# Four small row vectors loaded through GpSimd's queue, and their PE transpose placed later, in a gated state-space and MLP kernel

## The chip, the cores and the metric

The kernel runs on one core of a Trainium2 chip. Times are device microseconds of one execution. A smaller number, the **span**, runs from the first to the last instruction that the profile shows. The engines are PE (matmul; PEld is its weight load), DVE (vector), ACT (scalar), POOL (GpSimd) and SP (sync, here the main issuer of transfers).

## The reference, cut to what matters

```python
g = sigmoid((x * gate_w).sum(-1))                  # x: 2048 x 640, bf16
# branch A: a diagonal complex recurrence of 640 states along the 2048 steps
dt = exp(log_dt); Lam = Lambda_re + 1j * Lambda_im
Lam_bar = exp(dt * Lam)                            # needs exp, sin and cos of small vectors
B_bar = ((Lam_bar - 1) / Lam)[:, None] * (B_re + 1j * B_im)
h[t] = Lam_bar * h[t-1] + B_bar @ x[t]
a = 2 * real(C @ h) + x * Dskip
# branch B: an MLP of 1728 hidden units
b = gelu(x @ w1 + b1) @ w2 + b2
out = g * a + (1 - g) * b
```

The four small vectors of the title are `Lambda_re`, `Lambda_im`, `log_dt` (640 each) and the first 1664 elements of `b1`.

## The kernel before: the parts concerned

The vectors are loaded as rows of one 128 x 128 tile, 128 elements a row, and PE transposes the tile once, so that each vector lies down the partitions. The transpose borrows PSUM bank 7 before the MLP needs it.

```python
for i, (nm, (r0, src)) in enumerate(ROWS.items()):       # lre, lim, ldt, b1a
    src = src.rearrange("(k p) -> k p", p=128)
    load(nm, "act", "l_" + nm, rows[r0:r0 + src.shape[0], :], src, [nm], prio=-100 + i, dur=0.4)
load("b1b", "act", ...)                                  # the rest of b1, on ACT's queue in both kernels
...
psC = PS[7][:, :].bitcast(BF16)[:, 0:128]
op("cols", "pe", 0.3, list(ROWS) + ["b1b", "ident"], [("bank", 7)], f_cols, prio=13.5)   # the transpose
op("cols1", "dve", 0.2, [("bank", 7)], ["lcol", "b1col"], f_cols1, prio=-1000)           # its copy to SBUF
op("dt", "act", ...)      # exp(log_dt), then on DVE: angles; on ACT: two sines; on DVE: all tables
...
# the first MLP blocks: 42 matmuls, weight block k outermost, bank jf for hidden block jf
op(f"m1_0_{jf}_{k}_{t0}", "pe", ..., [("bank", jf)], f_mm, prio=pe_prio())   # prio 1, 2, 3, ...
op(f"ge_0_{jf}", "act", d_act(512), [("bank", jf), "b1col"], [("gl", 0, jf)], f_ge, prio=10)
...
# elsewhere: the next MLP block takes bank 0 again, so it waits for ge_0_0
```

`op` only registers an instruction. The builder then sorts each engine's instructions with its own estimates of durations (the third argument, `dur`, `lat`): at each step an engine takes the ready one of lowest `prio`. In the traces each engine runs its list in that order: the transpose comes after 13, 18 or 21 matmuls, just as the builder placed it.

## Time and profile before

| | before |
|---|---|
| median of the first three runs | 212.67 us (212.47 to 213.09) |
| span of the profiled run, a later one of 213.45 us | 212.1 us |
| PE busy | 98% |
| DVE busy | 90% |
| ACT busy | 49% |
| GpSimd busy | 2% |

The busy shares say which engine can't be made to wait: PE.

### The profile page before, as it was taken

The numbers are of one execution on the slowest core, as the hardware profiler recorded it, in microseconds if no ns is written. First come the engines' busy times: TensorE is split into PE (matmuls) and PEld (weight loads), VectorE is DVE, ScalarE is ACT, GpSimd is POOL, SyncE is SP. The second block draws the span as 40 slices with busy tenths as digits, with TensorE's granted clock in tenths as the row PEclk, the third lists the DMA queues.
The fourth block names the chain that finished last, engine by engine and source line by source line (L and its number), as shares of the span: only waits on it lengthen the run. The fifth ranks groups of instructions, "written<-read, shape, count | busy, mean of one in ns | idle before, by whom it ended". The sixth has DMA issues, their size and how long they took to land.

```text
span 212.1 us, 2737 instructions
## 1 busy us (share of the span) xinstructions
PE 208.0 (98%) x1088; PEld 104.9 (49%) x1102; DVE 190.1 (90%) x240; ACT 103.0 (49%) x177; POOL 4.2 (2%) x12
## 2 busy tenths in 40 slices
PE   7999999999999999999999999999999999999996
PEld 3444444444564444444464444444446444567775
DVE  2399999999999999999999999899999999499744
ACT  2389556677960353556681063455660027623330
POOL 1000000030000000000000000000010000000000
DMA  5999999999600010075274000004742000005251
GB/s 163 202 279 135 207 171 198 380 222 162 185 12 3 0 49 0 0 85 111 54 59 114 3 0 0 0 2 115 96 96 117 0 3 0 0 0 104 68 140 63
DMA packets 48808, 19.08 MB, mean 90 GB/s; under 512 B 41500, under 2 KB 47772, under 8 KB 48796
## 3 DMA queue, kind: packets, MB, share of 16 engines
q1 hardware_dynamic: 47136, 17.59, 39.7%
q0 software_dynamic: 1600, 1.32, 4.5%
q8 instruction: 8, 0.13, 0.4%
q14 instruction: 4, 0.03, 0.1%
q10 hardware_dynamic: 60, 0.01, 0.0%
HBM read 8.41 MB, written 2.63 MB: 52 GB/s over the span
## 4 chain that ended last, share of the span: by engine, by line
PE 96%; DMA 2%; issue 1%; SPq 0%; DVE 0%
PE ps L662 22%; PE ps L705 20%; PE ps L929 20%; PE ps L978 15%; PE ps L792 7%; PE ps L841 5%; PE ps L640 4%; DMA W1sb<-in_B_w_dram 2%; PE ps L683 1%; PE ps L940 1%; PE ps L806 0%; SPq L333 0%; DVE W1sb L875 0%; PE ps L446 0%
## 5 line engine op out<-in xcount | busy, mean ns | idle before, releaser
L662 PE MATMUL ps<-xT,W1sb 128*128 128x512 bf16 x215 | 47.5, 379 | 0.3
L745 DVE TENSOR_TENSOR_SCAN W<-atab,V 128x1280 bf16<-128x1280 f32 x16 | 44.3, 2812 | 0.3
L705 PE MATMUL ps<-xT,BT 128*128 128x512 bf16 x196 | 43.1, 379 | 0.3 <-issue 0.2
L929 PE MATMUL ps<-Gl,W2sb 128*128 128x512 bf16 (+1 forms) x230 | 42.5, 343 | 0.2
L669 ACT ACTIVATE Gl<-ps,cols 128x512 bf16<-128x512 f32 x44 | 29.9, 694 | 15.5 <-PE ps L662 15.5
L662 PEld LDWEIGHTS ps<-xT,W1sb 128*128 128x128 bf16 x220 | 21.6, 98 | 25.9
L978 PE MATMUL ps<-Hb,CT 128*128 128x512 bf16 x150 | 32.9, 379 | 0.0
L929 PEld LDWEIGHTS ps<-Gl,W2sb 128*128 128x128 bf16 x234 | 22.9, 98 | 19.3
L705 PEld LDWEIGHTS ps<-xT,BT 128*128 128x128 bf16 x200 | 19.5, 98 | 23.7 <-ACT Gt L691 0.4
L714 ACT ACTIVATE U<-ps 128x512 bf16<-128x512 f32 x40 | 23.6, 599 | 14.6 <-PE ps L705 14.5
L947 ACT ACTIVATE E1T<-ps,cols 128x512 bf16<-128x512 f32 (+1 forms) x18 | 9.5, 624 | 36.0 <-PE ps L940 36.0
L978 PEld LDWEIGHTS ps<-Hb,CT 128*128 128x128 bf16 x150 | 14.5, 98 | 17.9 <-DVE V L496 0.6
L986 ACT ACTIVATE E2T<-ps 128x512 bf16<-128x512 f32 x15 | 9.1, 604 | 13.6 <-PE ps L978 13.6
L792 PE MATMUL ps<-W2sb,Gl 128*128 128x320 bf16 x104 | 14.8, 299 | 0.0
L615 DVE SCALAR_TENSOR_TENSOR trf<-xn,gwb 128x640 bf16<-128x640 bf16 x16 | 13.2, 823 | 0.4
L496 DVE TENSOR_TENSOR V<-V,W 128x1280 bf16<-128x1280 bf16 x16 | 12.5, 822 | 0.3
L496 DVE TENSOR_TENSOR Hb<-Hb,V 128x1280 bf16<-128x1280 bf16 x16 | 12.5, 822 | 0.3
L496 DVE TENSOR_TENSOR V<-mr,U 128x2560 bf16<-128x2560 bf16 x8 | 11.9, 1492 | 0.3
L792 PEld LDWEIGHTS ps<-W2sb,Gl 128*128 128x128 bf16 x104 | 10.1, 98 | 4.3 <-issue 0.3
L496 DVE TENSOR_TENSOR Hb<-c,W 128x2560 bf16<-128x2560 bf16 x8 | 11.9, 1491 | 0.2
L496 DVE TENSOR_TENSOR W<-mi,U 128x2560 bf16<-128x2560 bf16 x8 | 11.9, 1484 | 0.0
L496 DVE TENSOR_TENSOR V<-s,W 128x2560 bf16<-128x2560 bf16 x8 | 11.9, 1484 | 0.0
(91 smaller groups left out, 150.8 us busy)
## 6 DMA issues: line engine op xcount, KB each, us to landing
W2sb<-in_B_w_dram SPq DMA_DIRECT2D x1, 2080.0 KB, 8.9
out_dram<-xn SPq DMA_DIRECT2D x3, 640.0 KB, 4.8
xn<-in_A_x_dram POOLq DMA_DIRECT2D x2, 640.0 KB, 7.3
W1sb<-in_B_w_dram SPq DMA_DIRECT2D x3, 256.0 KB, 3.7
trf<-grow SPq DMA_DIRECT2D x3, 256.0 KB, 5.3
xn<-in_A_x_dram SPq DMA_DIRECT2D x1, 640.0 KB, 7.7
W1sb<-in_B_w_dram SPq DMA_DIRECT2D x1, 480.0 KB, 4.6
out_dram<-W1sb SPq DMA_DIRECT2D x3, 160.0 KB, 1.8
```

The source lines that it names most:

```text
L496: return inc("dve", nc.vector.tensor_tensor(out=o, in0=a, in1=b, op=o_))
L615: t = inc("dve", nc.vector.scalar_tensor_tensor(out=scr[:, :], in0=xn[q % 2][:, c, :], scalar=1.0, in1=gwb[:, :], op0=ALU.mult, op1=ALU.mu ...
L662: t = nc.tensor.matmul(PS[bank][:, :], W1sb[:, k, jf * 128:(jf + 1) * 128], xT[q][:, k, :], start=(k == 0), stop=(k == KD - 1))
L669: return inc("act", nc.scalar.activation(Gl[q % 2][:, jf, :], PS[bank][:, :], ACT.Gelu_apprx_tanh, bias=b1col[:, jf:jf + 1]))
L705: t = nc.tensor.matmul(PS[bank][:, :], BT[:, ci, kd, k * 128:(k + 1) * 128], xT[q][:, kd, :], start=(kd == 0), stop=(kd == KD - 1))
L714: return inc("act", nc.scalar.activation(dst, src, ACT.Copy, scale=1.0 if ci == 0 else -1.0))
L745: t = inc("dve", nc.vector.tensor_tensor_scan(out=g[:, ci, :], data0=a, data1=v[:, ci, :], initial=0.0, op0=ALU.mult, op1=ALU.add))
L792: t = nc.tensor.matmul(PS[bank][:, 0:HALF], Gl[q % 2][:, jf, t4 * 128:(t4 + 1) * 128], W2sb[:, jf, cols], start=False, stop=False, skip_gr ...
L841: t = nc.tensor.matmul(PS[bank][:, 0:n], H[b % NHB][:, ci, k, s * 128:(s + 1) * 128], CT[:, ci, k, cols], start=(i == 0), stop=(i == 2 * K ...
L929: t = nc.tensor.matmul(PS[bank][:, 0:t1 - t0], W2sb[:, jf, d * 128:(d + 1) * 128], Gl[q % 2][:, jf, t0:t1], start=(jf == 0), stop=False)
L947: return inc("act", nc.scalar.activation(E1T[:, d, t0:t1], PS[bank][:, 0:t1 - t0], ACT.Identity, bias=cols2[:, 0, d:d + 1]))
L978: t = nc.tensor.matmul(PS[bank][:, :].rearrange("p (s t) -> p s t", s=2), CT[:, ci, k, d * 128:(d + 1) * 128], Hb[:, 2 * (q % 2):2 * (q % ...
```

## The change

The intent, as the edit and the builder's estimates show it: take four transfer issues of 0.31 us each off ACT's queue, where they delay ACT's first table load, and give them to GpSimd, which is idle; and since the builder reckons that GpSimd's loads arrive later, let PE do seven more matmuls before the transpose.

```diff
-            load(nm, "act", "l_" + nm, rows[r0:r0 + src.shape[0], :], src, [nm], prio=-100 + i, dur=0.4)
+            load(nm, "pool", "l_" + nm, rows[r0:r0 + src.shape[0], :], src, [nm], prio=-50 + i, dur=1.0)
...
-        op("cols", "pe", 0.3, list(ROWS) + ["b1b", "ident"], [("bank", 7)], f_cols, prio=13.5)
+        op("cols", "pe", 0.3, list(ROWS) + ["b1b", "ident"], [("bank", 7)], f_cols, prio=20.5)
```

## The prediction

> **What bounds the kernel now.** I read three views, in this order: the chain of work that ended last, the timeline of the first 16 us, and the timeline of DVE over the rest. The chain first:
>
> ```profile
> PE 96%; DMA 2%; issue 1%; SPq 0%; DVE 0%
> ```
>
> 96% of the span is matmuls following one another, and in its ordered form the only pieces that aren't PE or 0.05 us of issue are the start (the first W1 block, issued at 1.26 us, landing at 5.1) and the last DVE evictions. So a change counts only if it moves the first matmul of the main work (5.25 us), opens a hole in PE's stream later, or delays the tail. The change touches the first 10 us, so the timeline of those is next; columns are start us, duration us, engine, line, operation, and in brackets the idle time before it and what ended it:
>
> ```profile
> 1.26 0.14 POOL L398 IOTA st_i<- 128x17 int32 x1
> ...
> 2.20 0.31 ACTq L333 DMA_DIRECT2D rows<-in_A_Lambda_re_dram  x1
> ...
> 3.22 0.32 ACTq L333 DMA_DIRECT2D rows<-in_B_b_dram  x1
> 3.57 1.28 ACT L456 ACT_TABLE_LOAD   x1 [3.57 <-issue]
> ...
> 8.03 0.22 PE L446 MATMUL ps<-ident,rows 128*128 128x128 bf16 x1
> ...
> 8.28 0.19 DVE L451 CAST cols<-ps 128x29 f32<-128x29 bf16 x1 [3.22 <-PE ps L446]
> 8.51 0.21 ACT L456 ACTIVATE dtb<-cols 128x5 bf16<-128x5 f32 x1 [3.65 <-DVE cols L451]
> ...
> 11.19 1.28 ACT L649 ACT_TABLE_LOAD   x1
> ...
> 13.03 3.58 ACT L649 ACTIVATE Gl<-ps,cols 128x512 bf16<-128x512 f32 x6 [0.56 <-PE ps L640]
> ...
> 14.34 1.89 PE L662 MATMUL ps<-xT,W1sb 128*128 128x512 bf16 x8
> ```
>
> The transpose of the row tile (L446, 8.03 us) starts a serial chain: PE, DVE (columns), ACT (exp of log_dt), DVE (angles), ACT (a sine table, two sines), ACT (the gelu table, done at 11.19 + 1.28 = 12.47 us). Only then can ACT evict the first MLP bank. In this kernel it then idles 0.56 us, because the bank itself is finished only at 13.0. That eviction ends near 13.03 + 0.69 = 13.72 us (0.69 is the duration of a gelu eviction), and PE needs its bank again at 14.34 (L662, ninth MLP block, bank 0). So there are **two slacks in series**, 0.56 and 0.62 us, together about 1.2 us from the transpose to a PE stall.
>
> DVE hangs on the same transpose and shows no idle time of note from 8.3 us until these waits:
>
> ```profile
> 84.17 1.49 DVE L496 TENSOR_TENSOR xT<-xT,E2T 128x2560 bf16<-128x2560 bf16 x1 [0.37 <-ACT E2T L986]
> ...
> 134.60 1.49 DVE L496 TENSOR_TENSOR xT<-xT,E2T 128x2560 bf16<-128x2560 bf16 x1 [0.70 <-ACT E2T L986]
> ...
> 183.46 0.17 DVE L626 TENSOR_SCALAR gcol<-gth 128x4 f32<-128x4 f32 x1 [1.43 <-ACT gth L622]
> ```
>
> A late DVE chain therefore stays late until about 84 us, and loses 0.37, 0.70 and 1.43 us of its lateness there.
>
> **What the Trainium skill says.** "DMA: Bandwidth & Descriptors", section "Issuing engines are not separate DMA queues": transfers issued by ScalarE, SyncE or GpSimd run on the same 16 DMA engines, and several issuers save only issue time. The trace fits: the W1 blocks land 3.7 to 3.9 us after issue both while ACT issues its rows and after; the row packets (queue q10, 60 packets in all) are too few to matter. The same page, "Latency and other measured facts", gives about 0.6 us to the first byte for the hardware path and about 1 us for GpSimd's. The trace has it slower: the packet records put the first byte of the first xn load from GpSimd 1.5 us after its issue starts. "Perfetto Trace Analysis", section "DMA Instruction — SWDGE (GPSIMD)", says that a GpSimd transfer's recorded end is the end of descriptor generation, not of data; that fits 0.98 us recorded against 6.5 us to landing here:
>
> ```profile
> cols<-in_B_b_dram POOLq DMA_DIRECT2D x1, 2.5 KB, 6.5
> ```
>
> "ScalarE: Activation LUTs", section "What ACT_TABLE_LOAD costs", gives about 1283 ns for a load, as here, plus a drain of about 1380 ns for a switch; the trace shows no such gap (9.24 + 1.28 = 10.52, next activation 10.60), so I use 1.28.
>
> **The change part by part.**
> *Removed from ACT's queue:* four issues at 0.31 us, from 2.20 to 3.54 us. The exp table load moves up about 1.35 us, and then ACT waits 1.35 us longer for the columns. Worth 0.
>
> *Added to GpSimd's queue:* four issues after the iotas, from about 1.45 us. At 0.77 to 0.98 us each (the four GpSimd issues of this trace), they end at 4.5 to 5.4. The bytes of the last come 0.7 (first xn load) to 2.4 us (the scattered cols load, 3.4 us from issue to first packet) after its descriptors; with half a microsecond to move and signal, rows complete between 5.7 and 8.3 us, best estimate 6.8. In the kernel before, the last row packet is at 5.9 us. GpSimd does nothing else until 43 us, so its time is free.
>
> *The transpose moves back.* The builder sorts each engine's instructions by priority and by its own duration estimates. I take only the order from it. In priority order the transpose passes matmuls 14 to 20. But matmuls 17 and 18 write bank 7, the bank that the transpose borrows, so they can't pass it. The builder's estimate for GpSimd's loads (1.0 each from 1.2, then 2.5) says 7.7, so PE is filled with 14, 15, 16 and 19 to 23: **eight matmuls**, not seven. At 0.2155 us a matmul (20 in 4.32 us in the ordered chain) the transpose is issued at 8.03 + 8 x 0.2155 = 9.75 us. That is 1.5 us after even the late bound of the landing, so PE should not wait for the rows. PE's amount of work is unchanged. Bank 7's first matmul now comes one matmul after the transpose and must wait for DVE's copy: about 0.2 us of stall at 10.1 us.
>
> *The chain behind it.* From transpose to gelu table took 12.47 - 8.03 = 4.44 us, all serial. New: 9.75 + 4.44 = 14.19 us. The first bank is then ready long before, so the gelu starts at once, ends at 14.19 + 0.69 = 14.88, and with 0.05 us for the semaphore PE resumes at 14.93 instead of 14.34: **loss 0.59 us**. The 0.2 us stall before lies inside it: PE merely arrives at the same wait later. The next bank is no further wait: evictions follow every 0.59 us, PE needs one per 5 x 0.2155 = 1.08 us.
>
> *DVE's 1.7 us lateness.* The scan states are needed by the output matmuls at 72.61 us and ready at 68.37 (slack 4.2); the last pair is ready at 198.49 and needed at 204.67 (6.2). The list sort may put one combine and one scaling ahead of the last state update, at most about 4 us of that slack. So: 0.
>
> *Sum:* 212.67 + 0.59 = 213.26 us; I say 213.2.
>
> **The rivals.**
> 1. *The rows arrive after 9.75 us and PE, which runs in order, waits in front of the transpose.* For: the 6.5 us landing of the cols load; if each of four loads behaved so, the last would land at 4.2 + 6.5 = 10.7. Against: that load is 640 two-byte descriptors beside a large weight transfer, a row load is 5 to 13 descriptors of 256 bytes; xn from GpSimd brings its first byte in 1.5 us. Each microsecond of lateness is one microsecond of time: 214.2.
> 2. *All hidden.* If the transpose came only five matmuls later (1.08 us), both slacks would just absorb it: 212.7. For: the builder's order depends on when it thinks the rows land. Against: its own numbers give eight.
> 3. *Faster start.* Without ACT's issues, W1 or the DMA transposes of x get going earlier: 212.4. For: the first transpose's issue took 1.20 us beside ACT's issues, later ones 1.13 and 1.12. Against: the W1 block that releases PE was issued at 1.26, before the four row loads.
> 4. *DVE becomes the bound.* It is busy 90%. If its lateness reached an output matmul, up to 1.7 us: 214.4. Against: the slacks above.
>
> **Range and chances.** The central term is a difference of two measured times, and its uncertainty is one matmul either way in the order (0.2 us), a tenth or two for the restart, and the rows' landing. The runs of before spread from 212.47 to 213.09. I take 212.5 to 214.2. Two per cent is 4.3 us: for that the rows would have to land at about 13 us (3%). No mechanism gains 4 us (1%).
>
> **What would show it.** Right: GpSimd's four issues between 1.4 and 5.4 us; L446 at 9.6 to 9.9 us with no DMA wait in front of it; the gelu table load ending near 14.2; no PE wait before ACT's first gelu, but a PE wait for ACT of 0.4 to 0.6 us before L662; DVE's waits at 84 and 134 us gone or smaller, no wait of PE for the scan states. Wrong: PE or PEld waiting for the rows' DMA (rival 1), L446 less than 1.2 us later (rival 2), first L640 before 5.15 us (rival 3), a wait of L978 or L841 for DVE (rival 4).

## More of the kernel before

The page's part 3 lists the transfers by queue; its columns are packets, MB and share of the 16 transfer engines:

```profile
q0 software_dynamic: 1600, 1.32, 4.5%
...
q14 instruction: 4, 0.03, 0.1%
q10 hardware_dynamic: 60, 0.01, 0.0%
```

q10 is ACT's queue with the row loads, q0 GpSimd's. q14 fetches instructions, here in four packets of 8192 bytes.

## The result, and the profile after

The changed kernel took 214.28 us (median of 6, 213.52 to 214.42), the kernel before 212.80 (6). The ratio was 1.0063, 95% interval 1.0045 to 1.0081. Ratios here are the mean time of one kernel's fast runs over that of the other's fast runs of the same rounds, so not quite the ratio of the medians. That is within 2%, as predicted; the median lies 0.08 us above the predicted range, while the predicted base times the ratio, 212.67 x 1.0063 = 214.01 us, lies inside it.

The timeline of the first microseconds, to be held against the one in the prediction. First the line of the kernel before that shows the 13 matmuls ahead of the transpose, then the changed kernel:

```profile
5.25 2.94 PE L640 MATMUL ps<-xT,W1sb 128*128 128x256 bf16 x13 [0.52 <-DMA W1sb<-in_B_w_dram]
```

```profile
2.18 1.28 ACT L456 ACT_TABLE_LOAD   x1 [2.18 <-POOL st_i L398]
...
3.19 0.52 POOL L333 DMA_DIRECT2D rows<-in_B_b_dram  x1
...
4.58 5.04 PE L640 MATMUL ps<-xT,W1sb 128*128 128x256 bf16 x21
...
9.46 0.22 PE L446 MATMUL ps<-ident,rows 128*128 128x128 bf16 x1
...
9.71 0.19 DVE L451 CAST cols<-ps 128x29 f32<-128x29 bf16 x1 [4.61 <-PE ps L446]
...
9.96 4.00 PEld L640 LDWEIGHTS ps<-xT,W1sb 128*128 128x128 bf16 x20 [0.40 <-DVE cols L451]
...
12.62 1.28 ACT L649 ACT_TABLE_LOAD   x1
...
13.92 3.58 ACT L649 ACTIVATE Gl<-ps,cols 128x512 bf16<-128x512 f32 x6
...
14.75 2.53 PE L662 MATMUL ps<-xT,W1sb 128*128 128x512 bf16 x11 [0.30 <-ACT Gl L649]
```

ACT's table load moved up from 3.57 to 2.18 us, which gains nothing. GpSimd's last issue ends at 3.71. The transpose L446 sits behind 21 matmuls (13 before), with no wait for a transfer in front of it. The gelu table is ready at 12.62 + 1.28 = 13.90 us, the first gelu starts at once, and L662 waits for it. The transfer list gives the landings, in us from the start of the issue:

```profile
rows<-in_A_Lambda_re_dram POOLq DMA_DIRECT2D x1, 1.2 KB, 3.1
...
rows<-in_B_b_dram POOLq DMA_DIRECT2D x1, 3.2 KB, 3.3
```

So the last row is there at 3.19 + 3.3 = 6.5 us, three before the transpose. Its last packet is at 5.8 us; in the kernel before, with the rows on ACT's queue, the last one is at 5.9. So the rows were not late at all: the edited priority (18 matmuls, as five_later_padded shows below) and the builder's estimate of 7.7 us (21) put the transpose back, not GpSimd's loads. The chain of work that ended last now runs through ACT and DVE at its start:

```profile
PE 96%; ACT 1%; DVE 1%; issue 0%
```

In both traces the span is the start of L662 plus the same remainder: 212.13 - 14.34 = 197.79 and 212.54 - 14.75 = 197.79 us. So **inside the span, all that differs is decided before L662**, and none of DVE's lateness reaches PE. DVE's waits confirm this (the first of the three in the prediction is gone, the second shrank from 0.70 to 0.16, the third is as it was):

```profile
135.00 1.49 DVE L496 TENSOR_TENSOR xT<-xT,E2T 128x2560 bf16<-128x2560 bf16 x1 [0.16 <-ACT E2T L986]
...
183.87 0.17 DVE L626 TENSOR_SCALAR gcol<-gth 128x4 f32<-128x4 f32 x1 [1.44 <-ACT gth L622]
```

But the spans of the two traces differ by only 0.4 us where the times differ by 1.5. Part of that is chance before 8 us (when the first weights land), and part isn't in the span at all: the six runs of the changed kernel exceed their spans by 1.92, 1.89, 1.83, 1.42, 1.38 and 1.73 us, the profiled run of before by 1.35. The experiments had to separate the two.

### The profile page after: what moved, and what is told of

Its sections match the earlier page's. It is cut to its first block, busy times and chain, and to the rows that moved or that the text cites. A ratio compares the mean times of both kernels' runs of the same rounds, so it can differ in the third digit from the quotient of the medians.

```text
span 212.5 us, 2752 instructions
## 1 busy us (share of the span) xinstructions
PE 209.4 (99%) x1102; PEld 104.8 (49%) x1102; DVE 190.0 (89%) x240; ACT 102.9 (48%) x177; POOL 6.4 (3%) x16
## 3 DMA queue, kind: packets, MB, share of 16 engines
q0 software_dynamic: 1728, 1.32, 4.9%
## 4 chain that ended last, share of the span: by engine, by line
PE 96%; ACT 1%; DVE 1%; issue 0%
PE ps L662 22%; PE ps L705 20%; PE ps L929 20%; PE ps L978 15%; PE ps L792 7%; PE ps L841 5%; PE ps L640 2%; PE ps L415 1%; PE ps L683 1%; PE ps L940 1%; ACT L649 1%; PE ps L427 0%; ACT Gl L649 0%; PE ps L806 0%; DVE W1sb L875 0%
## 5 line engine op out<-in xcount | busy, mean ns | idle before, releaser
L662 PE MATMUL ps<-xT,W1sb 128*128 128x512 bf16 x220 | 48.1, 379 | 0.3 <-ACT Gl L649 0.3
L705 PE MATMUL ps<-xT,BT 128*128 128x512 bf16 x200 | 43.8, 379 | 0.0
L662 PEld LDWEIGHTS ps<-xT,W1sb 128*128 128x128 bf16 x220 | 21.4, 98 | 26.5 <-issue 0.8
```

Of the source, the lines that this page charges most:

```text
L662: t = nc.tensor.matmul(PS[bank][:, :], W1sb[:, k, jf * 128:(jf + 1) * 128], xT[q][:, k, :], start=(k == 0), stop=(k == KD - 1))
L705: t = nc.tensor.matmul(PS[bank][:, :], BT[:, ci, kd, k * 128:(k + 1) * 128], xT[q][:, kd, :], start=(kd == 0), stop=(kd == KD - 1))
```

## The experiments

All were timed in five rounds beside the kernel before on the same chip (six executions each, eleven of before). All results were right, that of the tanh kernel included, though it was made wrong (its difference stays within the tolerance). "Excess" is time minus span.

### The two halves of the change, apart

**same_as_before**: no edit.

> The kernel before under another name, as a control. All theories: ratio 1.000 within 0.001. Its trace is a second look at three things that one trace can't settle: when the first main matmul (L640) starts (5.25 us in the first trace; 4.58 in that of the changed kernel), the span (212.1), and by how much the measured time exceeds the span (1.35 us in the one profiled run of before, 1.4 to 1.9 in those of the changed kernel). If L640 again starts at 5.2 or later, the early start is an effect of the change; if it starts near 4.6, it is chance.

Ratio 1.0004 (0.9988 to 1.002), excess 1.30 to 1.38. L640, the first main matmul, started at 5.19 us here, which alone would have spoken for an effect of the change. But it started at 4.4 to 4.6 us in later kernels with the order of before and the rows on ACT's queue (four_spare_loads_later, 4.43; before_shortened, 4.52; five_empty_on_gpsimd, 4.61). So its early start in the changed kernel is chance, not an effect of emptying ACT's queue.

**loads_alone**: GpSimd's loads, and the builder told that they are short, so PE, DVE and ACT keep the order of before.

```diff
-  load(nm, "act", ..., prio=-100 + i, dur=0.4)
+  load(nm, "pool", ..., prio=-50 + i, dur=0.25)
```

> The four row loads on GpSimd's queue as in the change, but the builder is told that they are cheap, so every compute engine keeps the order of before (transpose after 13 matmuls). Theory A (the cost is the late transpose alone): ratio 1.000, span as before. Theory B (GpSimd's loads cost time outside the span, the late transpose costs little): ratio 1.003 to 1.006 at a span no longer than before, measured time minus span 1.8 us or more. Theory C (without ACT's loads the first weight block lands earlier): L640 starts at about 4.6, span 211.5, ratio 0.997.

Ratio 1.0017 (0.9997 to 1.0036). Excess 1.42, 1.76, 1.36, 1.33, 1.41, 1.83. Median span 211.7 beside 211.6 for before in the same rounds.

**late_transpose_alone**: the loads stay with ACT, and the builder is told that they land late, which gives PE, DVE and ACT the order of the changed kernel.

```diff
-  load(nm, "act", ..., dur=0.4)
+  load(nm, "act", ..., dur=0.4, lat=4.7)
-  op("cols", ..., prio=13.5)
+  op("cols", ..., prio=20.5)
```

> The row loads stay on ACT's queue; only the transpose moves, to after 21 matmuls, with every compute engine in the order of the changed kernel. Theory A: ratio 1.0028 to 1.006 and PE waits 0.4 to 0.6 us for ACT's first gelu before L662. Theory B: ratio about 1.002, measured time minus span as before (1.35). Theory C: L640 starts at 5.2, so the stall before L662 is only as long as the late chain makes it (0.6), span 212.7.

Ratio 1.0051 (1.0016 to 1.0087; one run of 215.91 widens it, the median is 213.6). Excess 1.31 to 1.38 in all six. Its trace shows the same two holes in PE's stream as the changed kernel's:

```profile
9.11 0.22 PE L446 MATMUL ps<-ident,rows 128*128 128x128 bf16 x1
...
9.61 4.00 PEld L640 LDWEIGHTS ps<-xT,W1sb 128*128 128x128 bf16 x20 [0.40 <-DVE cols L451]
...
14.41 0.81 PE L662 MATMUL ps<-xT,W1sb 128*128 128x512 bf16 x3 [0.30 <-ACT Gl L649]
```

**change_again**: the changed kernel.

> The changed kernel again, beside the other three on the same chip. All theories: ratio 1.0045 to 1.008. Theory A: equal to late_transpose_alone within 0.001. Theory B: its ratio is the product of the two parts, and its measured time minus span is 1.8 us, above that of late_transpose_alone. Theory C: L640 at 4.6 again and a span 0.6 us shorter than that of late_transpose_alone.

Ratio 1.0046 (1.0032 to 1.006), excess 1.84, 1.35, 1.38, 1.40, 1.89, 1.73.

What follows. From L446 to L662 the traces show 6.31 us with the transpose after 13 matmuls (before 14.34 - 8.03; same_as_before 13.88 - 7.57; loads_alone 14.05 - 7.73 = 6.32) and 5.29 or 5.30 after 21 (14.75 - 9.46, 14.41 - 9.11, 14.38 - 9.09). (Later traces with 13 have 6.32, 6.35 twice and once 6.76, in before_shortened, where the transpose came early, at 6.89, and L662 waited 0.5 us for its weights: 6.31 is the undisturbed distance.) Without a stall the latter would be 6.31 - 8 x 0.2155 = 4.59. **The late transpose costs PE 5.29 - 4.59 = 0.70 us.** The successive starts of PE's matmuls split it: 0.23 us behind the transpose (the second next matmul waits for DVE's copy out of bank 7) and 0.46 at L662 (the 0.30 in brackets counts from the modelled end of the matmul before). The loads on GpSimd's queue make no hole between the two, but with them the excess takes a second value, some 0.4 us higher, in part of the runs.

### What the excess is: two tests that tested nothing, and two that did

In before, the last 8 KB packet of q14 starts at 209.0 us. In both traces of the changed kernel it comes after the span (214.1 and 213.8), and in that of loads_alone it is missing. The window from 205 to 216 us in 40 slices of 0.275 us, GB/s moved in each; first before, then the changed kernel:

```profile
GB/s 0 0 0 0 0 0 0 0 0 0 0 0 0 0 30 0 0 88 363 145 0 82 339 153 22 0 0 0 0 0 0 0 0 0 0 0 0 0 0 0
```

```profile
GB/s 0 0 0 0 0 0 0 0 0 0 0 0 0 0 0 0 0 0 0 275 312 9 0 268 215 113 0 0 0 0 0 0 0 30 0 0 0 0 0 0
```

The lone 30 is the fetch: the fifteenth slice (209 us), ahead of the last stores, against the thirty-fourth (214), behind them. The two groups of large numbers are the stores. Two explanations: the fetch is ACT's, whose program is four instructions shorter (theory D), or the excess comes from GpSimd's queue (theory E).

**change_padded**: the changed kernel with four more empty instructions on ACT.

```diff
-  for _ in range(14 if q == NQ - 2 else 0):
+  for _ in range((14 + (4 if d == 0 else 0)) if q == NQ - 2 else 0):
       nc.scalar.nop(nofuse=True)
```

> The changed kernel plus four empty instructions on ACT at about 109 us, where ACT has time, so that ACT's program is again as long as before (409 instructions; the change made it 405). Every other instruction is the same. Theory D (the part of the loss outside the span is a late refill of ACT's instructions: the runtime's queue q14 fetched its last 8 KB at 209 us in before, and at 214 us, after the span, in the changed kernel): the q14 packet is back at about 209, measured time minus span is 1.35 us in every run, ratio 1.003. Theory E (it is GpSimd's queue, its four extra transfers or its 32 instructions instead of 27): measured time minus span stays at 1.4 to 1.9, ratio 1.0045 to 1.006.

Ratio 1.0028 (1.0015 to 1.0042), excess 1.40, 1.36, 1.32, 1.33, 1.43, 1.72; last fetch missing.

**before_shortened**: the kernel before with four empty ones fewer (`-4` in the same place).

> The kernel before with four of its empty ACT instructions fewer (405 in all), nothing else changed; GpSimd's queue as before. Theory D: span as before (211.6), but measured time minus span is 1.4 to 1.9 us in part of the runs, the last q14 packet lies behind the span or is missing, ratio about 1.001 to 1.002. Theory E: 1.35 us in every run, ratio 1.000.

Ratio 1.0013 (0.9993 to 1.0034), excess 1.28 to 1.36, fetch at 208.5. Both results spoke for theory E.

**five_empty_on_gpsimd**: the kernel before with five empty instructions on GpSimd.

```diff
+  for _ in range(5):
+      nc.gpsimd.nop(nofuse=True)
   return inc("pool", nc.gpsimd.iota(st_i[:, A1:NS], ...))
```

> The kernel before with five empty instructions on GpSimd before its last iota: GpSimd's program is as long as in the changed kernel (32 instructions instead of 27), without any further transfer. Theory F (the part outside the span comes from the length of GpSimd's program, the late 8 KB fetch of q14 being its own): measured time minus span lies at 1.4 or at 1.7 to 1.9 us in part of the runs, and the q14 packet at 209 us is gone or lies behind the span. Theory G (it comes from GpSimd's additional transfers): 1.28 to 1.39 in all six runs, q14 packet at 209, ratio 1.000.

Ratio 1.0006 (0.9962 to 1.005), excess 1.28 to 1.36, fetch at 208.4.

These three runs are misses of design: **the compiler removes the empty instructions**. The compiled ACT program has 192 instructions in before and before_shortened alike, 188 in the changed kernel and in change_padded; each pair is the same byte for byte. The runs are thus repeats of before and of the change, and no evidence for either theory.

**four_spare_loads_later**: before, with four more row loads from GpSimd at about 46 us into a tile that nobody reads. These do exist in the compiled program (25 instructions on GpSimd, as in the changed kernel; ACT has its 192).

```diff
+  spare = SB("spare", [5, 128], BF16)
+  for i in range(4):
+      load(f"spare{i}", "pool", f"l_spare{i}", spare[:, :], A_Lambda_re.rearrange(...), ["spare"], prio=-20 + i, dur=1.0, after=[big])
```

> The kernel before with four extra row loads from GpSimd into a spare tile that nobody reads, at about 46 us, after its other two small loads; rows and transpose as before. Theory G: measured time minus span at 1.4 or 1.7 to 1.9 in part of the runs, span as before (211.6), ratio 1.0005 to 1.002. If it takes early transfers to cause it (theory H): 1.28 to 1.39 in every run, ratio 1.000.

Ratio 0.9979 (0.9943 to 1.0016), excess 1.28 to 1.37, fetch at 208.4. So neither four more transfers from GpSimd nor its longer program brought the second value in six executions; early transfers still might.

**change_real_padding**: the changed kernel with five real activations of one element on ACT at 109 us, which bring its compiled program back to 192 instructions.

```diff
+  for i in range(5 if q == NQ - 2 and d == 0 else 0):
+      nc.scalar.activation(spare[0:1, i:i + 1], one[0:1, 0:1], ACT.Copy)
```

> The two earlier paddings tested nothing: the compiler removes empty instructions, as the sizes of the compiled ACT programs show (192 instructions in before and in before_shortened, 188 in the changed kernel and in change_padded; 191 in short_chain, whose last q14 fetch moved from 209 to 211 us). This is the changed kernel with five one-element activations on ACT at about 109 us, which bring its compiled program back to 192; order otherwise that of the change. Theory D (the excess outside the span comes from the place of ACT's last 8 KB fetch): q14 packet back at 209 us, measured time minus span 1.28 to 1.39 in all six runs, span 212.2 to 212.4, ratio 1.0028 to 1.0035. Theory H (it comes from transfers that GpSimd issues early): 1.4 or 1.7 to 1.9 in part of the runs, ratio 1.0045. In both: L446 to L662 5.29 us.

Excess 1.39, 1.27, 1.32, 1.36, 1.31, 1.36: the second value is gone, with the rows still on GpSimd's queue. The fetch is back:

```profile
GB/s 0 0 0 0 0 0 0 0 0 0 0 0 0 0 30 0 0 0 307 284 5 0 298 203 95 0 0 0 0 0 0 0 0 0 0 0 0 0 0 0
```

L446 to L662 is 14.44 - 9.16 = 5.28, ratio 1.002 (0.998 to 1.006; one run of before at 215.3 widens it), median 213.58 beside 212.94. This speaks for theory D and against theory H (early transfers), by six executions: the kernels with 188 ACT instructions had the second value in 14 of 36, and at those odds six without it would come by chance about once in twenty.

### How the loss grows, and what the chain consists of

**loads_alone_padded**: loads_alone with the empty instructions, so in fact a repeat of it.

> GpSimd's loads with the order of before, plus the four empty ACT instructions. Theory D: measured time minus span 1.35 us in every run, ratio 1.000 within 0.001 if the loads themselves cost nothing in the span, 1.001 if they delay the weights by the 0.2 us by which the mean span of loads_alone exceeded that of before. Theory E: 1.4 to 1.9 in part of the runs, ratio 1.0015.

Ratio 1.0008 (0.9993 to 1.0022), excess 1.35 to 1.42 and once 1.67, median span 211.65 beside 211.7. With loads_alone, which is the same program: GpSimd's loads cost nothing that can be told from zero within the span.

**five_later_padded**: the same loads, the transpose after 18 matmuls (`prio=20.5`).

> As loads_alone_padded, but the transpose five matmuls later instead of eight. Slack theory: from the transpose to L662 the undisturbed distance is 6.31 us after 13 matmuls, 6.31 - 5 x 0.2155 = 5.23 after 18; the serial chain needs 5.29 (measured in late_transpose_alone and both traces of the change). So PE loses 0.06 us: ratio 1.000 to 1.001, L446 to L662 5.29 us. If instead the loss grew with every matmul of delay, five eighths of 0.70: 0.44 us, ratio 1.002.

Its trace shows PE reaching L662 unhindered by ACT, yet 5.48 us after the transpose instead of 5.23:

```profile
8.42 0.22 PE L446 MATMUL ps<-ident,rows 128*128 128x128 bf16 x1
...
8.92 4.65 PEld L640 LDWEIGHTS ps<-xT,W1sb 128*128 128x128 bf16 x23 [0.40 <-DVE cols L451]
...
12.88 2.42 ACT L649 ACTIVATE Gl<-ps,cols 128x512 bf16<-128x512 f32 x4
...
13.90 1.46 PE L662 MATMUL ps<-xT,W1sb 128*128 128x512 bf16 x6
```

The first gelu ends at 12.88 + 0.69 = 13.57, before PE comes. The 0.25 us are the wait behind bank 7's copy (0.23 by the successive starts; the 0.40 us of weight-load idleness, where a weight load every 0.2155 us leaves half its time idle anyway), which here has no later wait to hide in. I had overlooked that: the expected 0.06 was wrong. The timed ratio was 1.0033 (1.0016 to 1.0049), more than 0.25 us: the excess was 1.37 to 1.41 three times and 1.66 to 1.70 three times, as its ACT program is short too (188), and the spans were 211.7, 211.9 and four times 212.3 or 212.4. Only the run of 211.7 has a trace, so **why four runs were 0.6 us longer stays open**. The times alone would fit the other theory (0.44 us) too; the trace speaks against its path, since nothing holds PE at L662.

**short_chain**: late_transpose_alone with `ACT.Tanh` for `ACT.Sin`.

> late_transpose_alone, but the two sines are replaced by tanh, which needs no table of its own: one table load of 1.28 us fewer in the chain between transpose and first gelu. The result is wrong on purpose. Chain theory (the late transpose costs because that chain ends after PE wants bank 0): PE no longer waits for ACT's first gelu; L446 to L662 falls from 5.29 us to 4.59 plus the wait for bank 7's copy (0.2), some 4.8; span 211.7 to 211.8, ratio 1.0005 to 1.001. Rival (the loss is PE's own reordering, such as waiting for the third weight block that it reaches earlier, and not the chain): 5.29 us and ratio 1.003 as in late_transpose_alone.

L446 to L662 stayed at 14.14 - 8.84 = 5.30 us. One table load was gone, but the chain was as long: ACT now waited for DVE.

```profile
11.06 0.33 DVE L484 SCALAR_TENSOR_TENSOR trf<-trf 128x165 f32<-128x165 f32 x1
...
11.42 0.34 ACT L489 ACTIVATE trf<-trf 128x165 f32<-128x165 f32 x1 [1.38 <-DVE trf L484]
```

The sine table had been loading beside DVE's five angle instructions, so taking it away shortened nothing. The run therefore doesn't tell the chain from its rival. The traces taken together do: in all six with 21 matmuls before the transpose (this one among them), L662 starts 0.14 to 0.15 us after the end of the first gelu, although L662 itself lies anywhere from 14.14 to 14.75 us. What releases PE there is the gelu, so the rival falls.

The run shows something else. Its ratio was 1.0073 (1.0034 to 1.0113) at an excess of 1.29 to 1.39: its ACT program has 191 instructions, the fetch starts at 211.15 us, and the last store lands late. In the packet records the fetch runs from 211.15 to 211.76 us; the store's packets pause from 211.49 on and go on at 211.76. The same transfer in the window from 205 us, us to landing last, in before and in short_chain:

```profile
out_dram<-W1sb SPq DMA_DIRECT2D x1, 32.0 KB, 1.5
```

```profile
out_dram<-W1sb SPq DMA_DIRECT2D x1, 32.0 KB, 2.1
```

Its span ends 212.50 - 14.14 = 198.36 us behind the start of L662, where 197.76 to 197.81 is the rule of the other thirteen traces: nearly 0.6 us more, with one instruction fewer. This is one trace, and the fastest of the six executions: the other five have spans of 213.0 to 214.6 us, which nothing here explains.

### The sums

| order of PE | rows on | ACT instructions | executions | median span | excess | of them over 1.6 |
|---|---|---|---|---|---|---|
| before | ACT | 192 | 68 | 211.6 | 1.27 to 1.39 | 0 |
| before | GpSimd | 188 | 12 | 211.65 | 1.33 to 1.83 | 3 |
| changed | ACT | 192 | 6 | 212.25 | 1.31 to 1.38 | 0 |
| changed | GpSimd | 188 | 18 | 212.3 | 1.32 to 1.92 | 8 |
| changed, real padding | GpSimd | 192 | 6 | 212.2 | 1.27 to 1.39 | 0 |
| transpose after 18 | GpSimd | 188 | 6 | 212.3 | 1.37 to 1.70 | 3 |
| changed, tanh for sine | ACT | 191 | 6 | 213.3 | 1.29 to 1.39 | 0 |

Over the 14 traces the last fetch goes with the length of ACT's program alone: it starts at 208.4 to 209.1 us in the seven with 192 instructions, at 211.15 in the one with 191, and in the six with 188 behind the span (twice) or not at all in the trace (four times).

The change costs 0.7 us within the span, all of it by the late transpose, and on average 0.25 us outside (mean excess of the 18 executions 1.57, of the 68 of before 1.32). Together 0.95 us, or 1.0045; the same compiled program measured 1.0063, 1.0046 and 1.0028 on three occasions. None of these kernels is measurably faster than the one before.

## Why the prediction was right or wrong

**The bound and the two slacks: right.** The time was decided where the prediction looked, and PE ran into the first gelu at L662. The absence of any loss later is shown by the constant 197.79 us.

**ACT's relief: right.** Worth nothing; ACT waited 6.5 us for the columns instead of 3.7.

**GpSimd's loads: right, on the safe side.** The issues took 0.52 to 0.68 us, not 0.77 to 0.98, and the rows were there at 6.5 us (6.8 predicted). Rival 1 never came near. Two readings on the way were off without harm: the 640 pieces of the cols load are packets of four bytes in the trace, not two, and the half microsecond to move and signal, which came from no line, is 0.7 us from the last row packet (5.8) to the landing.

**Eight matmuls: right.** 21 before the transpose instead of 13. L446 came at 9.46 us, not at 9.75, because the first weights landed earlier: PE began 0.68 us sooner and lost 0.36 of it again in two waits before its seventh matmul. That is luck, as the starts of the other kernels show.

**The chain: right in length, wrong in its parts.** From L446 to the end of the gelu table: 13.90 - 9.46 = 4.44 us, to the hundredth. But "all serial" was false: short_chain shows that the sine table load lies beside DVE's work and ends about when that does.

**The loss of 0.59 us: the mechanism held, the size was 0.70.** The mis-sized term is the restart: the prediction gave 0.05 us from the end of the gelu to L662, and the trace shows 14.75 - 13.92 - 0.69 = 0.14. So the two slacks together hold 6.31 - 5.29 = 1.02 us, not 1.2. That bank 7's wait of 0.2 us lies inside the loss was right for eight matmuls; five_later_padded shows it standing alone.

**The step that fell short is the last one, "Sum: 212.67 + 0.59".** It counted only what the span contains. Outside it came 0.25 us on average (0.37 in the first measurement, whose mean excess is 1.70), most likely by a side effect that the prediction didn't consider: with four instructions fewer on ACT its last instruction fetch no longer comes at 209 us, where nothing waits for it, but behind the span or not in the trace. This, and the particular rounds of the first measurement (1.34 us by ratio against 0.98 and 0.60 in two repeats), carried the median to 214.28.

**The rivals.** Of "all hidden", the trace of five_later_padded shows that even five matmuls weren't free, because of bank 7. "Faster start": its sign, a first L640 before 5.15 us, did appear (4.58), but it was no test, since the start varies from 4.43 to 5.25 us among kernels with the order of before and the rows on ACT's queue. "DVE becomes the bound" fell as argued: no output matmul waited longer for DVE than before. The predicted reordering in DVE's tail occurred (one combine and one scaling ahead of the last state update, which ended at 202.30 us instead of 198.49) and cost nothing.

What stays open: the long runs of five_later_padded and of short_chain, and why the second value, some 0.4 us more outside the span, comes in only part of the runs. Both traces with a fetch behind the span belong to runs with an excess of 1.84 or more, and the four traces of short ACT programs without it to runs of 1.38 to 1.42. That the fetch comes in exactly the long runs is likely, but six traces don't prove it.

## What to carry to other kernels

Moving work to an idle queue gains nothing if the engine that it leaves then waits for the same data; look for the wait that ends last, and add up the slacks in series from the moved instruction to the bound engine before moving it. Moving an instruction back in the list also brings it closer to the next user of a buffer that it borrows. Check the builder's estimate of a landing against the trace before letting it reorder the bound engine. And where a change alters the number of instructions on an engine, compare the time with the span, and check in the compiled program that padding is really there.

## What the Trainium skill lacked or had wrong

- "Runtime: NRT & Kernel Launch", section "Instruction fetch mechanics", says that instructions are refilled in 16 KiB blocks and that crossing a boundary is mostly hidden. The eight packets of q8 are indeed 16,384 bytes here, but ACT's refills on q14 are 8192 bytes. The last of them is hidden at 209 us, goes with nearly 0.6 us at 211 us beside the last store (one trace), and, where it is behind the span or missing, with some 0.4 us outside the span in part of the runs.
- No page that I read says that empty instructions don't reach the chip: the compiled ACT program kept 188 instructions with four added, and 192 with four removed.
- "DMA: Bandwidth & Descriptors", section "Anatomy of one DMA — SWDGE (gpsimd) path", puts a small GpSimd transfer at about 2.0 us; the four row loads of 1.2 to 3.2 KB took 3.1 to 3.5 us from the start of their issue to landing beside the weight loads, and 0.52 to 0.68 us of that was the issue.
- "ScalarE: Activation LUTs", section "What ACT_TABLE_LOAD costs": the 1283 ns are what the traces show; the drain of 1380 ns shows nowhere (gelu table load 12.62 + 1.28, first gelu at 13.92).
